# Three small products of a fused attention and MLP kernel: the second factor as a per-partition scalar operand

## The chip, the core and the metric

The kernel runs on one core of a Trainium2 chip. Its engines work side by side, each through its own queue in order: PE (TensorE, matrix products), DVE (VectorE), ACT (ScalarE), POOL (GpSimd), and SP (SyncE), whose queue here only issues transfers. The metric is the device time of one execution in microseconds (us). Three executions of the kernel before took 630.42 us (median), between 629.82 and 632.25.

## The reference

Three stages run one after the other. The first is an attention in which a query sees only the keys of its own cluster, the second an MLP with a gate, the third an MLP whose activation is a softmax-weighted value followed by a layer norm. The change lies in the third, of which this is the whole computation:

```python
h = x @ w_in                                  # 1536 x 512 times 512 x 1024
h_max = np.max(h, axis=-1, keepdims=True)
e = np.exp(h - h_max)
sm = e / (np.sum(e, axis=-1, keepdims=True) + 1e-09)
solu = h * sm
mu = np.mean(solu, axis=-1, keepdims=True)
var = np.mean((solu - mu) ** 2, axis=-1, keepdims=True)
ln = (solu - mu) / np.sqrt(var + 1e-06) * g_ln
return (ln @ w_out).astype(np.float32)        # 1536 x 1024 times 1024 x 512
```

## The kernel before

The attention and the first layer are put in order by a planner with costs and due times; the change doesn't touch them. The third stage is written out in the order in which each engine is to run it. Its 1536 tokens are 12 tiles of 128 (t = 0 to 11). All operands of the products are split into a high and a low f16 half, so each product takes three matmuls, and the values in PSUM still carry a power of two that is taken out by a scale, r, one number per partition.

For a tile t the work is in four functions:

- `products(t)` (L1365): 24 matmuls on PE, which fill two PSUM tiles h of 128x512.
- `solu(t, hs)`, first part. DVE takes the maximum of each half, negated (L1376, twice), and the smaller of the two (L1378), and multiplies it by r (L1379): this is nm. ACT computes exp(r*h + nm) with its sum (L1383, twice). DVE adds the sums (L1385), takes the reciprocal (L1388), multiplies it by r (L1389), and multiplies exp, this factor and h (L1392, twice); then the mean mu (L1396).
- `solu(t, hs)`, second part. ACT squares and sums (L1402), DVE makes the variance (L1404), POOL its power -1/2 (L1406), DVE scales it (L1407) and normalises (L1408, 128x1024). ACT copies the result to f16, the high half (L1410), and POOL subtracts that from the full value, the low half (L1412, two inputs of 128x1024 f32 and f16 in SBUF). For the last tile DVE does this subtraction.
- `flip(t, lh)` transposes both halves by two DMAs from SP's queue (L1420); for the last tile PE transposes them (L1425) and DVE copies them out of PSUM (L1426). `store(t, lT)` is 24 matmuls (L1441, for the last tile twice 24 of half the width), a copy out of PSUM on ACT (L1449) and the DMA to the output (L1450).

`factor(t)` makes the scale r once for every three tiles (L1356), in four calls.

The loop at L1487 runs, for each t, `products(t)`, then `flip(t - 2)` and `store(t - 3)`, then all of `solu(t)`. On PE the 24 matmuls of `products(t)` therefore stand right ahead of the 24 of `store(t - 3)`. On ACT the copy L1449 of tile t - 3 stands behind L1410 of tile t - 1 and ahead of the two L1383 of tile t. On DVE the maxima L1376 of tile t stand right behind L1408 of tile t - 1. On SP the output DMA of tile t - 2 stands ahead of the two transposing DMAs of tile t. Tiles 0 and 1 are computed earlier, between parts of the second stage, and for the last tile the second part of `solu` comes one turn later.

Of the kernel before, what the change touches and what calls it, by code (L numbers as in the profile page):

```python
# [15 lines left out]
ALU = mybir.AluOpType  # L16
# [5 lines left out]
def kernel(  # L22
# [21 lines left out]
    nc = tc.nc  # L44
# [82 lines left out]
    def scalar():  # L127
        i = n_scl[0]
        n_scl[0] += 1
        return scl[:, i:i + 1]  # L130
# [650 lines left out]
    def values():  # L781
# [45 lines left out]
        a = add(dict(PE=0.1), XDUE, longest_sum, after=[a], take="ex")  # L827
        add(dict(DVE=1.1), XDUE, lambda t, a=a: x_power(a), after=[a, scales["v"]], frees=a)
        T["VF"] = add(dict(DVE=0.1), 8, lambda t: factor(), after=list(scales.values()))
        for p in range(NH // 2):  # L830

# [465 lines left out]
    w2 = Weight(2, w2_in, "w2", reg1[:, 0:10])  # L1297
# [8 lines left out]
    rho, rho2, rests = [], {}, []  # L1306
# [44 lines left out]
    def factor(t):  # L1351

        n = t * P // TB
        if n not in rho2:
            rho2[n] = scalar()
            nc.vector.tensor_tensor(out=rho2[n], in0=rho[n], in1=w2.i, op=ALU.mult)  # L1356
        return rho2[n]

    def products(t):
# [11 lines left out]

    def solu(t, hs):
        r = factor(t)
        m2 = s_p.tile([P, 2], F32, tag="m2", name="m2")
        for h, _, i in hs:
            nc.vector.tensor_reduce(out=m2[:, i], in_=h, op=ALU.max, axis=AX.X, negate=True)  # L1376
        nm = s_p.tile([P, 1], F32, tag="nm2", name="nm2")
        nc.vector.tensor_reduce(out=nm, in_=m2, op=ALU.min, axis=AX.X)  # L1378
        nc.vector.tensor_tensor(out=nm, in0=nm, in1=r, op=ALU.mult)  # L1379
        e = slots[:, t % NL, :]  # L1380
        sm = s_p.tile([P, 2], F32, tag="sm2", name="sm2")
        for h, s, i in hs:
            nc.scalar.activation(e[:, s], h, AF.Exp, bias=nm, scale=r, accum_out=sm[:, i])  # L1383
        ri = s_p.tile([P, 1], F32, tag="ri2", name="ri2")
        nc.vector.tensor_scalar(  # L1385
            out=ri, in0=sm[:, 0:1], scalar1=sm[:, 1:2], scalar2=1e-9, op0=ALU.add, op1=ALU.add
        )
        nc.vector.reciprocal(ri, ri)  # L1388
        nc.vector.tensor_tensor(out=ri, in0=ri, in1=r, op=ALU.mult)  # L1389
        tot = s_p.tile([P, 2], F32, tag="tot", name="tot")  # L1390
        for h, s, i in hs:
            nc.vector.scalar_tensor_tensor(  # L1392
                out=e[:, s], in0=e[:, s], scalar=ri, in1=h, op0=ALU.mult, op1=ALU.mult, accum_out=tot[:, i]
            )
        mu = s_p.tile([P, 1], F32, tag="mu", name="mu")
        nc.vector.tensor_scalar(  # L1396
            out=mu, in0=tot[:, 0:1], scalar1=tot[:, 1:2], scalar2=-1.0 / FF2, op0=ALU.add, op1=ALU.mult
        )
        yield
        ln = slots[:, NL + t % NL, :]  # L1400
        vs = s_p.tile([P, 1], F32, tag="vs", name="vs")
        nc.scalar.activation(ln, e, AF.Square, bias=mu, accum_out=vs)  # L1402
        va = s_p.tile([P, 1], F32, tag="va2", name="va2")
        nc.vector.tensor_scalar(out=va, in0=vs, scalar1=1.0 / FF2, scalar2=1e-6, op0=ALU.mult, op1=ALU.add)  # L1404
        rs = s_p.tile([P, 1], F32, tag="rs", name="rs")
        nc.gpsimd.tensor_tensor(out=rs, in0=va, in1=mhalf, op=ALU.pow)  # L1406
        nc.vector.tensor_scalar_mul(rs, rs, LN)  # L1407
        nc.vector.tensor_scalar(out=ln, in0=e, scalar1=mu, scalar2=rs, op0=ALU.add, op1=ALU.mult)  # L1408
        lh = halves[:, t % NL]
        nc.scalar.copy(lh[:, 0], ln)  # L1410
        low = nc.gpsimd if t < NT - 1 else nc.vector
        low.tensor_tensor(out=lh[:, 1], in0=ln, in1=lh[:, 0], op=ALU.subtract)  # L1412
        lns[t] = lh
        yield
# [39 lines left out]
    def early(c):  # L1454

        if 0 < c < 3:
            while w2.done < w2.n:
                advance(fill)
            for _ in solu(c - 1, products(c - 1)):
                pass  # L1460
# [26 lines left out]
    for t in range(2, NT + 4):  # L1487
        hs = products(t) if t < NT else None
        if t == 2:
            rests.pop()()  # L1490
        part = store(t - 3, lts.pop(t - 3)) if 0 <= t - 3 < NT else iter(())
        if t >= NT:
            next(part, None)
        if t - 2 < NT:
            lts[t - 2] = flip(t - 2, lns[t - 2])
        if t == NT:
            next(last)
        for _ in part:
            pass
        if hs:  # L1500
            last = solu(t, hs)
            next(last)
            if t < NT - 1:
                next(last)
# [30 lines left out]
```

## Time and profile before

| | |
|---|---|
| Median of three runs | 630.42 us (629.82 to 632.25) |
| The profiled execution's own time | 631.68 us |
| Its span, first to last instruction | 629.9 us |
| Busy in the span: PE, DVE, ACT, POOL | 604.0, 456.9, 391.8, 250.0 us |
| Share of the span | 96%, 73%, 62%, 40% |

The profile is one execution. A row of the timeline gives the start from the span's beginning, the duration, the engine, the source line, the operation, what is written and read with shapes, the number of instructions merged into the row, and in brackets how long the engine had been idle and who ended that. A row of a source line gives the minimum, median and maximum duration of its instructions. Matmul ends are modelled: 24 matmuls of 512 columns are shown as 5.34 us, and the next group starts 5.18 us after them. The third stage without the work of the second is the stretch from 508.96 us to the end.

### The profile page before, as it was taken

How to read it: one execution, taken by the hardware profiler on the slowest of the kernel's cores; microseconds unless marked ns; L12 is line 12 of the kernel's file. 1: busy time of each engine (PE TensorE's matmuls, PEld its weight loads, DVE VectorE, ACT ScalarE, POOL GpSimd, SP SyncE). 2: the span in 40 equal slices, each digit the busy share in tenths (PEclk: the TensorE clock that was granted, in tenths of full speed). 3: DMA queues.
4: the chain of work that ended last, by engine and by line, in shares of the span. 5: the costliest groups of instructions: out<-in, count | busy, mean ns of one | idle time of the engine just before them, and what ended most of it. 6: DMA issues, size and time to landing. Idle time of an engine off the chain costs nothing. (4 is left out here: it accounts for less than half of the span.)

```text
span 629.9 us, 12832 instructions
## 1 busy us (share of the span) xinstructions
PE 604.0 (96%) x4879; PEld 395.5 (63%) x4879; DVE 456.9 (73%) x1003; ACT 391.8 (62%) x782; POOL 250.0 (40%) x215
## 2 busy tenths in 40 slices
PE   7989999999999989999999999999999999999977
PEld 6767787888888765556654666666665544444424
DVE  6878989999898858999988033566866356566662
ACT  3589998999999986678777035435335334443432
POOL 8139998758678971224221015200000212222220
PEclk9998999999999999999999999999999999999989
DMA  5897977879797116444520000260500312524241
GB/s 139 203 234 154 211 150 172 191 168 192 163 189 166 44 39 169 143 139 163 170 99 1 1 2 2 67 199 3 167 1 1 34 34 54 98 50 101 51 101 50
DMA packets 78786, 67.93 MB, mean 108 GB/s; under 512 B 61642, under 2 KB 64548, under 8 KB 78724
## 3 DMA queue, kind: packets, MB, share of 16 engines
q1 hardware_dynamic: 78724, 67.11, 44.9%
q8 instruction: 38, 0.62, 0.4%
q14 instruction: 24, 0.20, 0.1%
HBM read 34.64 MB, written 3.15 MB: 60 GB/s over the span
## 5 line engine op out<-in xcount | busy, mean ns | idle before, releaser
L976 POOL TENSOR_TENSOR ph<-p,ph 128x512 f16<-128x512 f32 x115 | 139.4, 1233 | 49.2 <-ACT ph L972 28.4
L1316 PE MATMUL yps<-g,reg 128*128 128x384 f16 x768 | 127.6, 326 | 1.0 <-DVE reg L232 0.9
L1156 PE MATMUL hps<-xT,reg 128*128 128x384 f16 x768 | 126.2, 326 | 1.5 <-DVE g L1167 1.5
L1316 PEld LDWEIGHTS <-reg 128*128 128x128 f16 x768 | 74.7, 98 | 52.4 <-DVE reg L232 4.4
L1156 PEld LDWEIGHTS <-reg 128*128 128x128 f16 x768 | 75.0, 98 | 50.5 <-issue 1.7
L914 DVE TENSOR_REDUCE nma<-sm 128x1 f32<-128x512 f32 x144 | 96.3, 680 | 8.4 <-PE sm L903 7.8
L1177 POOL TENSOR_TENSOR g<-g,g 128x384 f16<-128x384 f32 x40 | 41.7, 1044 | 123.8 <-ACT g L1172 123.8
L967 ACT ACTIVATE p<-st 128x512 f32<-128x512 f32 x114 | 68.6, 609 | 6.4 <-PE st L959 5.2
L958 PE MATMUL st<-OP 128*128 128x256 f32 (+1 forms) x191 | 69.3, 374 | 2.5 <-ACT p L967 1.3
L1406 POOL TENSOR_TENSOR rs<-va,mhalf 128x1 f32<-128x1 f32 x12 | 6.6, 551 | 158.9 <-DVE va L1404 158.9
L972 ACT CAST ph<-p 128x512 f16<-128x512 f32 x109 | 67.4, 630 | 0.4
L1365 PE MATMUL h<-reg,xT 128*128 128x512 f16 x288 | 64.1, 379 | 0.0
L959 PE MATMUL st<-OP 97*128 97x512 f32 (+3 forms) x191 | 63.0, 342 | 0.0
L995 PE MATMUL av<-vh,ph 128*128 128x65 f16 x576 | 61.1, 195 | 1.6 <-POOL ph L976 1.6
L991 PE MATMUL av<-vh,ph 128*128 128x65 f16 x576 | 61.9, 194 | 0.0
L994 PE MATMUL av<-vh,ph 128*128 128x64 f16 x576 | 61.2, 193 | 0.0
L991 PEld LDWEIGHTS <-ph 128*128 128x128 f16 x576 | 52.8, 99 | 11.2 <-issue 9.5
L903 PE MATMUL sm<-OP 80*128 80x512 f32 x192 | 57.6, 361 | 1.6 <-DVE nma L914 0.8
L1441 PEld LDWEIGHTS <-g 128*128 128x128 f16 x312 | 30.7, 99 | 39.0 <-DMA g<-g 6.6
L995 PEld LDWEIGHTS <-ph 128*128 128x128 f16 x576 | 53.6, 97 | 2.0 <-POOL ph L976 2.0
L994 PEld LDWEIGHTS <-ph 128*128 128x128 f16 x576 | 53.7, 97 | 0.2
L208 ACT ACTIVATE junk<-reg 128x512 bf16<-128x512 f32 x48 | 30.4, 633 | 30.8 <-DVE reg L198 18.6
(193 smaller groups left out, 1067.6 us busy)
## 6 DMA issues: line engine op xcount, KB each, us to landing
OP<-hl SPq DMA_DIRECT2D x48, 384.0 KB
raw<-in_moe_w_in_dram SPq DMA_DIRECT2D x24, 512.0 KB
raw<-in_moe_w_out_dram SPq DMA_DIRECT2D x24, 512.0 KB
xT<-in_v_dram SPq DMA_DIRECT2D x8, 384.0 KB
out_dram<-ob SPq DMA_DIRECT2D x11, 256.0 KB
raw<-in_k_dram SPq DMA_DIRECT2D x14, 192.0 KB
raw<-in_q_dram SPq DMA_DIRECT2D x14, 192.0 KB
OP<-oht SPq DMA_DIRECT2D x30, 48.0 KB
```

What stands on the lines that cost most here:

```text
L914: nc.vector.tensor_reduce(out=out, in_=src, op=ALU.max, axis=AX.X, negate=True)
L958: nc.tensor.matmul(t["tile"][:, at], K2[:, ks], Q2[:, cs], start=True, stop=False)
L959: nc.tensor.matmul(t["tile"][:, at], K1[0:n, ks], Q1[0:n, cs], start=False, stop=True)
L967: nc.scalar.activation(p32s[u, m], t["tile"], AF.Exp, scale=SCALE)
L972: e(phs[u, m][:, 0], p32s[u, m])
L976: e.tensor_tensor(out=phs[u, m][:, 1], in0=p32s.pop((u, m)), in1=phs[u, m][:, 0], op=ALU.subtract)
L991: nc.tensor.matmul(av[:, i, :], ph[:, 0, qs], vh[:, u, kt, D:], start=(m == 0 and i == 0), stop=False,)
L994: nc.tensor.matmul(av[:, i, 0:D], ph[:, 0, qs], vh[:, u, kt, 0:D], start=False, stop=False)
L995: nc.tensor.matmul(av[:, i, :], ph[:, 1, qs], vh[:, u, kt, D:], start=False, stop=(m == NU - 1 and kt == NJ - 1 and i == NJ - 1),)
L1156: nc.tensor.matmul(self.ps, w1.at(c, m, e), xT[:, x, c, n * TB:(n + 1) * TB], start=(c == 0 and e == x), stop=(c == ND - 1 and e == 1),)
L1316: nc.tensor.matmul(yps, wo.at(f, c, e), lp["g", n][:, x, f, :], start=(f == 0 and e == x), stop=(f == NF - 1 and e == 1),)
L1365: nc.tensor.matmul(h, xT[:, x, c, t * P:(t + 1) * P], w2.half(i * ND + c, e), start=(c == 0 and e == x), stop=(c == ND - 1 and x == 1),)
```

## The change

In `factor` and in two places of `solu`, a product of two 128x1 columns was a `tensor_tensor`, which reads both columns as tensors. It is now a `tensor_scalar_mul`, which reads one column as a tensor and the other as a scalar operand with one value per partition. The number and the order of the instructions on every engine stay as they were: 28 DVE instructions (4 at L1356, 12 at L1379, 12 at L1389) have another operation.

```diff
@@ factor(t)
             rho2[n] = scalar()
-            nc.vector.tensor_tensor(out=rho2[n], in0=rho[n], in1=w2.i, op=ALU.mult)
+            nc.vector.tensor_scalar_mul(rho2[n], rho[n], w2.i)
@@ solu(t, hs)
         nc.vector.tensor_reduce(out=nm, in_=m2, op=ALU.min, axis=AX.X)
-        nc.vector.tensor_tensor(out=nm, in0=nm, in1=r, op=ALU.mult)
+        nc.vector.tensor_scalar_mul(nm, nm, r)
...
         nc.vector.reciprocal(ri, ri)
-        nc.vector.tensor_tensor(out=ri, in0=ri, in1=r, op=ALU.mult)
+        nc.vector.tensor_scalar_mul(ri, ri, r)
```

## Rows read from the trace of the kernel before

**Rows 1.** Waits of PE from 520 to 630: who for whom, total, times, longest

```profile
PE ops__8220 L1441 <- DMA g<-g: 4.6, 2, 4.3
```

**Rows 2.** Timeline of PE: products of tile 11, stores of tiles 8 and 9

```profile
591.84 5.34 PE L1365 MATMUL h<-reg,xT 128*128 128x512 f16 x24
597.02 5.34 PE L1441 MATMUL ops__8134<-reg,g 128*128 128x512 f16 x24
602.20 5.60 PE L1441 MATMUL ops__8180<-reg,g 128*128 128x512 f16 x24
```

**Rows 3.** Timeline of DVE: the maxima of tiles 2 and 3

```profile
513.32 1.28 DVE L1376 TENSOR_REDUCE m<-h 128x1 f32<-128x512 f32 x2
...
522.17 1.28 DVE L1376 TENSOR_REDUCE m<-h 128x1 f32<-128x512 f32 x2
```

**Rows 4.** Two changed lines: durations minimum/median/maximum in ns, first and last start

```profile
L1379 DVE TENSOR_TENSOR nm<-nm,scl x12: 159/1896/1933, 484.0 to 608.1; 128x1 f32<-128x1 f32 x12
...
L1389 DVE TENSOR_TENSOR ri<-ri,scl x12: 159/159/161, 486.3 to 612.2; 128x1 f32<-128x1 f32 x12
```

**Rows 5.** Timeline of all engines, tile 8: from the maxima to exp

```profile
574.95 1.28 DVE L1376 TENSOR_REDUCE m<-h 128x1 f32<-128x512 f32 x2
...
576.24 2.13 POOL L1412 TENSOR_TENSOR g<-g,g 128x1024 f16<-128x1024 f32 x1 [2.25 <-issue]
...
576.45 1.93 DVE L1379 TENSOR_TENSOR nm<-nm,scl 128x1 f32<-128x1 f32 x1
...
578.42 0.78 ACT L1383 ACTIVATE g<-h,nm,scl 128x512 f32<-128x512 f32 x1 [1.72 <-DVE nm L1379]
```

**Rows 6.** Timeline, three earlier places: small TENSOR_SCALAR on DVE beside POOL

```profile
275.40 1.14 POOL L1177 TENSOR_TENSOR g<-g,g 128x384 f16<-128x384 f32 x1 [2.23 <-ACT g L1172]
...
276.17 0.20 DVE L1137 TENSOR_SCALAR scl<-scl 128x1 f32<-128x1 f32 x1
...
218.70 3.89 POOL L976 TENSOR_TENSOR ph<-p,ph 128x512 f16<-128x512 f32 x3
...
221.15 0.15 DVE L143 TENSOR_SCALAR scl<-scl 128x1 uint32<-128x1 uint32 x1
...
65.38 1.61 POOL L769 TENSOR_TENSOR vh<-xT,vh 128x768 f16<-128x768 f32 x1
...
66.42 0.59 DVE L1010 TENSOR_SCALAR ri<-ri,scl 128x6 f32<-128x6 f32 x1
```

**Rows 7.** Two TENSOR_SCALAR lines: L1385 with a scalar column, L1407 with a constant

```profile
L1385 DVE TENSOR_SCALAR ri<-sm x12: 212/214/215, 485.8 to 611.7; 128x1 f32<-128x1 f32 x12
...
L1407 DVE TENSOR_SCALAR rs<-rs x12: 154/154/155, 490.3 to 616.2; 128x1 f32<-128x1 f32 x12
```

**Rows 8.** Timeline of all engines, from the maxima of tile 11 on

```profile
606.61 1.28 DVE L1376 TENSOR_REDUCE m<-h 128x1 f32<-128x512 f32 x2
...
607.69 0.68 ACT L1449 ACTIVATE ob<-ops__8134,scl 128x512 f32<-128x512 f32 x1
...
608.82 2.68 SPq L1420 DMA_TRANSPOSE g<-g  x2
...
610.08 0.78 ACT L1383 ACTIVATE g<-h,nm,scl 128x512 f32<-128x512 f32 x1 [1.71 <-DVE nm L1379]
...
612.12 1.04 PE L1441 MATMUL ops__8220<-reg,g 128*128 128x512 f16 x2 [4.32 <-DMA g<-g]
...
613.47 5.44 PE L1441 MATMUL ops__8220<-reg,g 128*128 128x512 f16 x16 [0.31 <-DMA g<-g]
...
618.36 1.23 DVE L1412 TENSOR_TENSOR g<-g,g 128x1024 f16<-128x1024 f32 x1 [1.11 <-ACT g L1410]
...
621.40 2.78 PE L1441 MATMUL ops__8268<-reg,g 128*128 128x256 f16 x24
...
624.27 0.47 ACT L1449 ACTIVATE ob<-ops__8268,scl 128x256 f32<-128x256 f32 x1 [1.93 <-PE ops__8268 L1441]
```

**Rows 9.** Stretches: us, busy PE, PEld, DVE, ACT, POOL, PE clock, DMA, GB/s

```profile
607.00:612.00 5.00, 0.80 (x4) 0.19 (x2) 3.20 (x6) 3.00 (x6) 2.12 (x1) 0.83 0.55 127
612.00:614.00 2.00, 1.57 (x4) 0.39 (x5) 1.89 (x7) 0.00 (x0) 0.00 (x0) 0.50 0.41 76
```

## The prediction

> **What bounds the kernel now.** I read the page first, then PE's waits in the last stage, then the timeline by tile, and last the changed lines. On the page PE is busy 96% of the span, and from 520 us on PE waits only for the transposing DMA of tile 10, 4.6 us in two waits near the end [rows 1]. So one might call PE the bound. The timeline says otherwise for the last tiles. PE runs `products(t)` and `store(t - 3)` in turn, 5.18 us each (591.84, 597.02, 602.20), 10.36 us for a tile [rows 2]. DVE starts the maxima of tile 3 at 522.17 and those of tile 11 at 606.61: 84.44 us for eight tiles, 10.56 each [rows 3, 8]. PE had the products of tile 11 done at 591.84 + 5.34 = 597.2, and DVE comes to them 9.4 us later. PE runs ahead on work that it has in stock, and pays for it at the end, when it stands until 612.12 because tile 10 isn't normalised and transposed yet [rows 8]. From tile 3 on, the loop through DVE and ACT is what sets the end, not PE.
>
> **What the loop holds.** From tile 2 to tile 3 the maxima are 522.17 - 513.32 = 8.85 us apart [rows 3], later 10.56. The changed line L1379 explains the difference: of its 12 instructions the shortest takes 159 ns and the median 1896 [rows 4]. The timeline of tile 8 shows why. POOL's subtraction L1412 of the tile before starts at 576.24 and ends at 578.37; L1379, a product of 128x1, starts 0.21 us later and ends at 578.38, with it [rows 5]. ACT's exp waits for it and starts at 578.42. L1379 is held for as long as POOL's instruction runs. The median says that at least half of the tiles are held so; in the timeline it is nine of them, tiles 3 to 11, since for tiles 0 to 2 no subtraction runs at that moment. L1389, the same operation at a time when POOL is idle, takes 159 to 161 ns in all 12 cases.
>
> **The change part by part.** The question is whether the new form is held too.
>
> Rows bearing on it: L1137, an f32 TENSOR_SCALAR of 128x1 with a scalar column as the new ones have, takes 0.20 us at 276.17, while POOL's TENSOR_TENSOR runs from 275.40 to 276.54 [rows 6]. L143, 128x1 with a constant, takes 0.15 us at 221.15 inside three POOL subtractions that run without a gap from 218.70 to 222.59 [rows 6]. Against them stands L1010, a TENSOR_SCALAR of 128x6 with a scalar column: 0.59 us at 66.42, ending at 67.01 as POOL's subtraction ends at 66.99 [rows 6]. Wide ones are held, those of one element per partition are not, as far as these rows go.
>
> [...]
>
> The price of the new form itself: 0.154 us with a constant (L1407), 0.214 us with a scalar column (L1385) [rows 7], against 0.159 before. These are the two ends, -0.005 and +0.055 us an instruction. I take +0.055, since the new operand is a scalar column. Held, L1379 costs 1.93 us; free, 0.21. Each of nine tiles loses 1.72 us of the loop.
>
> L1356, four times 0.15 us before tiles 0, 3, 6 and 9, is on the loop in front of a tile and costs 4 x 0.055 = 0.2 us at most. Once PE sets the pace the slack of the loop hides this. L1389 stands between exp and the end of the tile: it costs 0.055 us, hidden by the same slack in every tile but the last.
>
> **What is late next.** Without the hold the DVE loop takes 8.85 + 2 x 0.055 = 8.96 us a tile, less than PE's 10.36, so something that goes with PE takes over. In the last tile's terms:
>
> - DVE alone: exp of tile 3 would start at 522.17 + 1.50 (from the maxima to L1379, as 574.95 to 576.45 [rows 5]) + 0.21 + 0.04 = 523.9, and exp of tile 11 eight loops later at 595.6.
> - ACT's order: the copy L1449 of tile t - 3 stands ahead of exp of tile t (before: 607.69, then 610.08 [rows 8]). It needs the store's matmuls, and PE runs these right behind `products(t)`. For tile 11 they end at 597.02 + 5.34 = 602.36 [rows 2]. ACT follows a PE group after 0.09 us (621.40 + 2.78 = 624.18, start 624.27 [rows 8]): L1449 from 602.45 to 603.13, exp of tile 11 from 603.1.
>
> The later one counts: 603.1 in place of 610.08, **7.0 us earlier**. The floor lies 10.36 us apart for successive tiles and the free loop 8.96, so counting back from tile 11 (7.5 us of distance, 1.4 lost per tile) the floor is in force from tile 6 on; the gain is limited by it and not by nine times 1.72 = 15.5 us.
>
> From exp of tile 11 to the end the chain has no other supplier: sums, L1392, square, variance, normalising, copy, the last subtraction (618.36 to 619.59), PE's transposes and the stores. It moves as a whole, less 0.055 us for L1389: 6.9 us. What could hold it up is PE's store of tile 10. PE is free of tile 9's store at 602.20 + 5.34 = 607.5. Tile 10's transposing DMA is issued 1.13 us after the start of L1449 (607.69 to 608.82 [rows 8]), so at 602.45 + 1.13 = 603.6; its first half lets PE go 3.30 us later and its second half 4.65 us later (612.12, 613.47 [rows 8]), at 606.9 and 608.2. The remaining 16 of the 18 matmuls ahead of the transposes are done at 608.2 + 16 x 0.216 = 611.7, with 0.216 = 5.18 / 24. The low half of tile 11 is ready at 619.59 - 6.9 = 612.7. PE is there first by 1 us, less the first eight transposes (at most 0.6). So nothing is lost there.
>
> **The sum.** Span 629.9 - 6.9 = 623.0, the profiled execution 631.68 - 6.9 = 624.8. The median of the runs shown lies 1.26 us under that execution: 630.42 - 6.9 = 623.5 us.
>
> **The rivals.**
>
> 1. The hold stays: a TENSOR_SCALAR of one element takes the shared path as the 128x6 one did. Place: L1379 beside L1412 in nine tiles. The DVE loop stays the bound, and each tile pays 2 x 0.055 us, 9 x 0.11 = 1.0 us: **631.4 us**, slower than before. It decides from the point at which one element per partition is held at all. For it: L1010. Against it: L1137 and L143. The change then does nothing but swap the operation. I give it 10%.
> 2. PE was the bound all along, and only the last tile's own 1.72 us, on the chain behind the last products, come off: **628.7 us**. For it: PE's 96% and no PE wait before the end. Against: 9.4 us between PE's end and DVE's start on tile 11, and the two pitches. 4%.
> 3. The gain comes but PE's clock takes half of it back. [...] In the forecast PE still stands about 0.4 us ahead of tile 10's second half. [...] 6%.
>
> **How the numbers follow.** The forecast has 80%: 623.5 us, 1.1% less. A difference under 0.5% (3.2 us) can't be told from none in a measurement of this kernel. Forecast and rival 3 lie beyond it on the fast side; rivals 1 and 2 inside it, rival 1 with a little chance of more. Faster 0.86, same 0.12, slower 0.02. The forecast's own spread: 0.4 us of the floor on ACT and of PE's end towards faster, 1 us in tile 10's transposes towards slower, and 1 us for the median of a few runs, since the three shown are spread over 2.4 us. With rival 3 taken in on the upper side, the range is 621.8 to 626.5.
>
> **What would show it.** In the profile of the changed kernel L1379 should take 0.15 to 0.22 us in all 12 cases, also while L1412 runs. The pitch of the maxima should be about 8.9 us for tiles 3 to 5 and 10.36 after, with ACT's exp waiting no longer for DVE but starting right behind L1449, which then waits for PE. Exp of tile 11 should start near 603.1, PE should wait under 1 us for tile 10's DMA where it waited 4.6, and the clock of 612 to 616 should read near 1. The forecast is wrong if L1379 still shows 1.9 us (rival 1), if it is short and the pitch stays at 10.56 (a new wait in the loop), or if PE starts tile 10's store early and slowly (rival 3).

## Result and profile after

The changed kernel takes 625.6 us (median of 20 runs, 623.53 to 631.09), the kernel before, measured beside it, 632.12 us (20 runs, 629.82 to 636.73). The ratio is 0.9897, with a 95% interval of 0.9876 to 0.9918: 1.0% faster, or 6.5 us, between 5.2 and 7.8. The forecast was 623.5 us, 6.9 us less. The profiled execution has a span of 622.7 us, where the forecast had 623.0.

First the two changed lines, minimum/median/maximum in ns; they answer to [rows 4].

```profile
L1379 DVE TENSOR_SCALAR nm<-nm,scl x12: 212/214/216, 483.5 to 600.8; 128x1 f32<-128x1 f32 x12
...
L1389 DVE TENSOR_SCALAR ri<-ri,scl x12: 212/214/215, 485.8 to 604.6; 128x1 f32<-128x1 f32 x12
```

L1379 is short in all 12 tiles. L1389, which was never held, has become 0.055 us longer. The wait of ACT's exp for L1379 is gone. Before, it was this (total, number of waits, longest):

```profile
ACT g L1383 <- DVE nm L1379: 15.5, 9, 1.8
```

Now tile 8 in the timeline after, from the maxima to exp; this answers to [rows 5].

```profile
568.20 1.28 DVE L1376 TENSOR_REDUCE m<-h 128x1 f32<-128x512 f32 x2
...
569.49 2.12 POOL L1412 TENSOR_TENSOR g<-g,g 128x1024 f16<-128x1024 f32 x1 [2.25 <-issue]
...
569.70 0.21 DVE L1379 TENSOR_SCALAR nm<-nm,scl 128x1 f32<-128x1 f32 x1
...
570.84 0.69 ACT L1449 ACTIVATE ob<-ops__7881,scl 128x512 f32<-128x512 f32 x1 [1.49 <-PE ops__7881 L1441]
...
571.43 0.77 ACT L1383 ACTIVATE g<-h,nm,scl 128x512 f32<-128x512 f32 x1
```

POOL's subtraction still runs for 2.12 us, and L1379 starts 0.21 us after it, as before. It now ends 1.70 us ahead of POOL. The wait of ACT has a new name: exp stands behind the copy L1449, and that waits 1.49 us for PE's store.

The maxima of tiles 3, 4, 7, 8 and 11 on DVE show two phases of the loop, where it was 10.56 us a tile before [rows 3, 8].

```profile
521.80 1.28 DVE L1376 TENSOR_REDUCE m<-h 128x1 f32<-128x512 f32 x2
...
530.69 1.28 DVE L1376 TENSOR_REDUCE m<-h 128x1 f32<-128x512 f32 x2
...
557.83 1.28 DVE L1376 TENSOR_REDUCE m<-h 128x1 f32<-128x512 f32 x2
568.20 1.28 DVE L1376 TENSOR_REDUCE m<-h 128x1 f32<-128x512 f32 x2
...
599.28 1.28 DVE L1376 TENSOR_REDUCE m<-h 128x1 f32<-128x512 f32 x2
```

From tile 3 to tile 4 it is 8.89 us, from tile 7 to tile 11 (599.28 - 557.83) / 4 = 10.36 on average, PE's pitch. Tile 11 starts 7.3 us earlier than before (606.61, [rows 8]).

The end, all engines, answers to the rest of [rows 8], and the wait of PE (first row) to [rows 1].

```profile
PE ops__8220 L1441 <- DMA g<-g: 0.9, 2, 0.7
```

```profile
601.92 0.69 ACT L1449 ACTIVATE ob<-ops__8134,scl 128x512 f32<-128x512 f32 x1 [1.48 <-PE ops__8134 L1441]
602.51 0.77 ACT L1383 ACTIVATE g<-h,nm,scl 128x512 f32<-128x512 f32 x1
...
603.06 3.53 SPq L1420 DMA_TRANSPOSE g<-g  x2
...
607.22 0.60 PE L1441 MATMUL ops__8220<-reg,g 128*128 128x512 f16 x2 [0.20 <-DMA g<-g]
...
608.52 3.63 PE L1441 MATMUL ops__8220<-reg,g 128*128 128x512 f16 x16 [0.70 <-DMA g<-g]
...
610.83 1.23 DVE L1412 TENSOR_TENSOR g<-g,g 128x1024 f16<-128x1024 f32 x1 [1.11 <-ACT g L1410]
...
611.99 1.06 PE L1425 MATMUL trl<-id,g 128*128 128x128 f16 x16
...
612.88 1.46 PE L1441 MATMUL ops__8220<-reg,g 128*128 128x512 f16 x6
```

The last row, the rest of tile 10's store behind the transposes, was this in the kernel before:

```profile
620.10 1.46 PE L1441 MATMUL ops__8220<-reg,g 128*128 128x512 f16 x6
```

PE's wait has gone from 4.6 to 0.9 us, and 16 matmuls take 3.63 us where they took 5.44. The stretch around the wait shows the clock, as in [rows 9] (us, busy PE, PEld, DVE, ACT, POOL, clock, DMA, GB/s): 1.00 after, 0.50 before.

```profile
607.00:609.00 2.00, 1.10 (x6) 0.36 (x6) 0.40 (x3) 0.87 (x2) 0.55 (x1) 1.00 0.47 86
```

**A yardstick for the experiments.** Ahead of tile 3, about the first 508 us, no changed instruction was held (they took 0.150 to 0.161 us each there before, 0.202 to 0.216 after), and the length of that part varies by up to 7 us between the profiles below. So I also compare the time from the first matmul of tile 3's products (start of its row on PE) to the end of the span. I call it the stage. Before it is 629.9 - 508.96 = 120.94 us; after, 622.7 - 508.44 = 114.26 us: 6.7 us less. Of the 7.2 us by which the spans differ, 0.5 lie ahead of the stage. Each stage comes from one profile; the changed kernel's two differ by 0.4 us, so differences of that size say nothing by themselves.

| kernel | tile 3 starts | span | stage | ratio to before (95%) |
|---|---|---|---|---|
| before | 508.96 | 629.9 | 120.9 | |
| the change | 508.44 | 622.7 | 114.3 | 0.9897 (0.9876 to 0.9918) |
| only L1379 | 511.53 | 625.6 | 114.1 | 0.9888 (0.9848 to 0.9928) |
| all but L1379 | 507.39 | 628.8 | 121.4 | 0.9987 (0.9965 to 1.0009) |
| last two tiles | 509.32 | 627.4 | 118.1 | 0.9948 (0.9923 to 0.9973) |
| all tiles but the last | 506.99 | 621.4 | 114.4 | 0.9857 (0.9822 to 0.9891) |
| one input in PSUM | 510.14 | 624.5 | 114.4 | 0.9895 (0.9839 to 0.9950) |
| scalar form, 2 columns | 509.82 | 630.8 | 121.0 | 1.0002 (0.9969 to 1.0035) |
| scalar form, 3 columns | 509.32 | 630.3 | 121.0 | 0.9991 (0.9965 to 1.0017) |
| copy late | 510.19 | 624.5 | 114.3 | 0.9877 (0.9839 to 0.9915) |
| copy late, DMA early | 509.55 | 622.5 | 113.0 | 0.9865 (0.9827 to 0.9903) |
| the change again | 513.91 | 628.6 | 114.7 | 0.9905 (0.9867 to 0.9942) |

### The profile page after: what moved, and what is told of

Same layout as the page of the kernel before. It is cut to its first block, busy times and chain, and to the rows that moved or that the text cites. A ratio compares the mean times of both kernels' runs of the same rounds, so it can differ in the third digit from the quotient of the medians.

```text
span 622.7 us, 12832 instructions
## 1 busy us (share of the span) xinstructions
PE 601.1 (97%) x4879; PEld 394.5 (63%) x4879; DVE 442.3 (71%) x1003; ACT 391.1 (63%) x782; POOL 250.0 (40%) x215
## 4 chain that ended last, share of the span: by engine, by line
PE 46%; DVE 10%; ACT 3%; issue 2%; DMA 1%; SPq 0%; ACTq 0%
PE yps L1316 19%; PE h L1365 10%; PE hps L1156 8%; DVE reg L198 2%; DVE g L1167 2%; DVE reg L232 1%; DVE reg L194 1%; DVE hps L1167 1%; DVE g L1177 1%; DVE reg L189 1%; ACT reg L229 1%; PE ops__8134 L1441 1%; PE ops__8050 L1441 1%; PE ops__7965 L1441 1%; PE ops__7881 L1441 1%
## 5 line engine op out<-in xcount | busy, mean ns | idle before, releaser
L1156 PE MATMUL hps<-xT,reg 128*128 128x384 f16 x768 | 127.9, 329 | 1.6 <-DVE g L1167 1.6
```

The source lines that it names most:

```text
L1156: nc.tensor.matmul(self.ps, w1.at(c, m, e), xT[:, x, c, n * TB:(n + 1) * TB], start=(c == 0 and e == x), stop=(c == ND - 1 and e == 1),)
```

## Experiments

**Which of the three lines.** Two kernels split the change.

```diff
 only L1379:
-        nc.vector.tensor_tensor(out=nm, in0=nm, in1=r, op=ALU.mult)
+        nc.vector.tensor_scalar_mul(nm, nm, r)
 all but L1379: the edits at L1356 and L1389, and L1379 as before
```

> Only L1379 (the product of the maximum with the scale) takes the scalar operand; L1356 and L1389 stay tensor products. My theory (L1379 was held behind POOL's L1412 for 1.7 us in nine tiles, the DVE loop set the end): the whole gain, 6.5 to 7 us, ratio about 0.9895; L1379 at 0.21 us in all tiles. Rival (the gain is spread over all 28 replaced instructions, or comes from L1389 and L1356): a part of it, under 4 us.

> L1356 and L1389 take the scalar operand, L1379 stays a tensor product. My theory: no gain, L1379 still 1.9 us in tiles 3 to 11; 9 x 0.055 = 0.5 us slower for the scalar operand at L1389, which a measurement can't tell from none. Rival (gain from these two lines): 3 us or more faster.

L1379 alone gives all of it: 0.9888, and 114.1 us in the stage. The other two lines give nothing: 0.9987, an interval that holds 1, and a stage that is 0.5 us longer, which fits 9 x 0.055 but is about what two profiles of one kernel differ by. From the maxima of tile 3 to those of tile 11 that kernel takes 605.48 - 520.70 = 84.78 us where the kernel before takes 84.44, 0.34 more where 8 x 0.055 makes 0.44. L1379 is held in that kernel as it was.

```profile
L1379 DVE TENSOR_TENSOR nm<-nm,scl x12: 159/1866/1930, 482.4 to 607.0; 128x1 f32<-128x1 f32 x12
```

**Loop or last tile.** If PE were the bound, the hold would count in the last tile alone.

```diff
-        nc.vector.tensor_tensor(out=nm, in0=nm, in1=r, op=ALU.mult)
+        if t >= NT - 2:            # the other kernel: t < NT - 1
+            nc.vector.tensor_scalar_mul(nm, nm, r)
+        else:
+            nc.vector.tensor_tensor(out=nm, in0=nm, in1=r, op=ALU.mult)
```

> L1379 takes the scalar operand in tiles 10 and 11 alone. My theory: the DVE loop sets the end in every tile, so each freed tile gives 1.67 us (1.72 less 0.05): 2 x 1.7 = 3.4 us faster, ratio 0.9946. Rival (PE is the bound and only the chain of the last tile counts): 1.7 us faster, ratio 0.997.

> L1379 takes the scalar operand in all tiles but the last, which keeps the tensor product. My theory: the loop catches up before the last tile, and there exp waits for ACT's copy of an older tile anyway; the changed kernel has nm ready 1.5 us ahead of exp, so a hold that ends with L1412 (602.7 in the changed kernel's profile) delays exp by about 0.2 us: 6.5 to 7 us faster, within 0.5 us of the full change. Rival (only the last tile's hold counts): no gain.

Freeing all tiles but the last gives the full gain (114.4 us), which refutes the last tile's hold as the cause. By the times it gives even more, 0.9857, 6.9 to 11.3 us; its stage doesn't show more than the full change. The added lines move what stands behind them by three: L1382 is the product of L1379, L1452 the copy L1449, L1386 the exp L1383. DVE of that kernel shows the last tile held for its 1.93 us, and ACT's exp behind it at 601.25, 0.08 us after the copy's end (in the changed kernel it starts 0.1 us ahead of that end): the hold is still there and costs about 0.1 to 0.2 us.

```profile
599.28 1.93 DVE L1382 TENSOR_TENSOR nm<-nm,scl 128x1 f32<-128x1 f32 x1
...
600.48 0.69 ACT L1452 ACTIVATE ob<-ops__8134,scl 128x512 f32<-128x512 f32 x1 [1.54 <-PE ops__8134 L1444]
...
601.25 0.78 ACT L1386 ACTIVATE g<-h,nm,scl 128x512 f32<-128x512 f32 x1
```

Freeing the last two gives 2.9 us in the stage, more than one tile's 1.7, and less than the 3.4 expected. The ratio, 0.9948, fits 3.3 us, but its interval reaches from 1.7 to 4.9 us and tells nothing here. Exp of tile 11 is where the theory puts it: 606.96 - 509.32 = 97.6 us after tile 3's products begin, 3.5 us earlier than before (610.08 - 508.96 = 101.1). The rest is lost on PE. These are exp of tile 11, PE's store of tile 10, and the stretch in which its second part starts.

```profile
606.96 0.78 ACT L1386 ACTIVATE g<-h,nm,scl 128x512 f32<-128x512 f32 x1
...
610.70 0.73 PE L1444 MATMUL ops__8220<-reg,g 128*128 128x512 f16 x2 [2.62 <-DVE g L1395]
612.03 4.81 PE L1444 MATMUL ops__8220<-reg,g 128*128 128x512 f16 x16 [0.60 <-DMA g<-g]
...
616.68 1.06 PE L1428 MATMUL trl<-id,g 128*128 128x128 f16 x16
```

```profile
612.00:614.00 2.00, 1.97 (x5) 0.73 (x6) 1.00 (x3) 0.27 (x2) 0.55 (x1) 0.50 0.00 0
```

PE had stood for 2.6 us (the row names a DVE instruction that ended just then, but PE starts 3.30 us after the issue of tile 10's transposing DMAs at 607.40, as before, 608.82 to 612.12 [rows 8], so I take these for what it waited for). From 612 to 614 the granted clock is 0.50, where the changed kernel has 1.00 during this store, and the 16 matmuls take 4.81 us, 1.2 us more than the 3.63 of the changed kernel; the transposes come behind them. I read the missing 0.6 us (3.5 less 2.9) as this. No run took the low clock away alone, so its share is argued, not shown.

**What is held: the operation or the second input.** In one kernel the product stays a TENSOR_TENSOR and one input moves. The product stands at L1380 there.

```diff
-        nc.vector.tensor_reduce(out=nm, in_=m2, op=ALU.min, axis=AX.X)
-        nc.vector.tensor_tensor(out=nm, in0=nm, in1=r, op=ALU.mult)
+        low_ = ps_c.tile([P, 512], F32, tag="acc", name="nmp")[:, 0:1]      # PSUM
+        nc.vector.tensor_reduce(out=low_, in_=m2, op=ALU.min, axis=AX.X)
+        nc.vector.tensor_tensor(out=nm, in0=low_, in1=r, op=ALU.mult)
```

> L1379 stays a tensor product, but the minimum (L1378) is written to PSUM, so that only one of the two inputs lies in SBUF. My theory (what is held is the second input from SBUF): L1379 under 0.3 us in all tiles, 6 to 7 us faster. Rival (the operation tensor_tensor is held, wherever its inputs lie): L1379 still 1.9 us, time as before.

```profile
L1380 DVE TENSOR_TENSOR nm<-nmp,scl x12: 157/159/159, 485.2 to 602.4; 128x1 f32<-128x1 f32 x12
```

The tensor product with one input in PSUM takes 0.16 us in all tiles, and the stage is 114.4 us. POOL's subtraction stands in that kernel as it did. In the changed kernel it starts 0.13 us after ACT's copy of the high half ends (600.45 to 600.58); with one input in PSUM that copy ends at 602.08 for tile 10, and tile 11's product starts at 602.4. By that estimate the two run side by side, as before. The operation alone wasn't held (0.16 us); with both its tensor inputs in SBUF it was (1.86 to 1.93 us in tiles 3 to 11 before).

**How wide may the scalar form be.** The edit writes the product two or three times, side by side; exp reads the first column. The product stands at L1380 here too.

```diff
-        nc.vector.tensor_tensor(out=nm, in0=nm, in1=r, op=ALU.mult)
+        wide = s_p.tile([P, 2], F32, tag="nmw", name="nmw")                 # or 3
+        nc.vector.tensor_scalar_mul(wide, nm.to_broadcast([P, 2]), r)
+        nm = wide[:, 0:1]
```

> L1379 is a product with a scalar operand as in the change, but over two columns (the minimum read twice, written to 128x2). Theory from the rows (one element per partition is free, wider ones take the second path as the 128x6 did): held, 1.9 us in tiles 3 to 11, time as before or up to 0.5 us more. Rival (the scalar form of such small width is free as such): 0.22 us, 6 to 7 us faster.

> The same over three columns. [...]

The first row is the kernel with two columns, the second that with three.

```profile
L1380 DVE TENSOR_SCALAR nmw<-nm,scl x12: 228/1902/1942, 484.8 to 609.1; 128x2 f32<-128x2 f32 x12
```

```profile
L1380 DVE TENSOR_SCALAR nmw<-nm,scl x12: 228/1900/1942, 484.3 to 608.6; 128x3 f32<-128x3 f32 x12
```

Both are held for 1.9 us, and the gain is gone (1.0002 and 0.9991, 121.0 us). One column more, and the change would have done nothing. POOL's subtraction of tile 7 ends at 579.31 with two columns and at 578.82 with three, the product of tile 8 beside it at 579.34 and 578.84. So 2 and 3 columns were held here, and the 6 of L1010, 0.59 us and ending 0.02 us after POOL's instruction [rows 6]; 1 column was not, 0.212 to 0.216 us at L1379 after the change and 0.20 at L1137 [rows 6]. What makes the difference is not shown.

**What sets the end now.** Two variants of the changed kernel, and the changed kernel once more.

```diff
 copy late: on ACT the copy L1449 of tile t - 3 behind the two exp of tile t
+        if hs:
+            last = solu(t, hs)
+            next(last)
         for _ in part:
             pass
         if hs:
-            last = solu(t, hs)
-            next(last)
             if t < NT - 1:
...
 DMA early, besides: tile 10's transposing DMAs ahead of tile 8's output DMA
-        if t - 2 < NT:
+        if t - 2 < NT and t - 2 not in lts:
...
+        if t == NT - 1:
+            lts[t - 1] = flip(t - 1, lns[t - 1])
         for _ in part:
```

> The changed kernel with ACT's copy L1449 of tile t - 3 put behind the two exp of tile t, not ahead of them. My theory (in the changed kernel exp waits for this copy, and the copy for PE's store): exp of tile 11 starts about 4.4 us earlier than in the changed kernel, right behind nm, but tile 10's transposing DMAs still stand behind the output DMA of tile 8, so PE's store of tile 10 starts as late as before: end at most 0.3 us earlier, time as the changed kernel. Rival (exp of the last tile alone sets the end): 4 us faster than the changed kernel.

> The same, and tile 10's transposing DMAs issued ahead of tile 8's output DMA. My theory: PE no longer waits at the end, 1.2 to 1.4 us less from the products of tile 3 to the end than the changed kernel: 0.2%, at the edge of what a measurement tells. Rival (the end hangs on something else by now): no difference from the changed kernel.

> The changed kernel itself, on the chip of the two variants: 6.5 to 7 us faster than before. Products of tile 3 to the end: 114.3 us, as in its first profile.

With the copy late, exp of tile 11 starts at 599.67, 89.5 us after tile 3's products, where the changed kernel has 602.51 - 508.44 = 94.1: 4.6 us earlier, right behind nm. The stage is as long as before it, 114.3 us, since PE still waits 1.0 us for tile 10's DMA.

```profile
599.67 0.78 ACT L1383 ACTIVATE g<-h,nm,scl 128x512 f32<-128x512 f32 x1 [1.61 <-DVE nm L1379]
...
604.82 3.61 SPq L1420 DMA_TRANSPOSE g<-g  x2
...
609.05 0.60 PE L1441 MATMUL ops__8220<-reg,g 128*128 128x512 f16 x2 [0.28 <-DMA g<-g]
610.33 3.63 PE L1441 MATMUL ops__8220<-reg,g 128*128 128x512 f16 x16 [0.67 <-DMA g<-g]
```

With the DMA early as well, PE runs the last three stores (that of tile 8 starts at 597.60) without a wait.

```profile
602.78 5.34 PE L1441 MATMUL ops__8182<-reg,g 128*128 128x512 f16 x24
607.96 4.05 PE L1441 MATMUL ops__8220<-reg,g 128*128 128x512 f16 x18
611.85 1.06 PE L1425 MATMUL trl<-id,g 128*128 128x128 f16 x16
```

The stage is 113.0 us, 1.3 us under the changed kernel's first profile and 1.7 under its second. The times don't settle it: medians of 624.29 against 626.79 us on that chip, and intervals of the ratios to before that overlap. By the profile this kernel beats both; by the times it is only no worse. The changed kernel's second measurement, 0.9905, agrees with its first (0.9897); its stage is 114.7 us, 0.4 above what was expected.

## Why the prediction was right

- **The hold.** L1379 was to take 0.15 to 0.22 us in 12 tiles; it takes 0.212 to 0.216. That the old form is held for its second tensor input from SBUF and the new one is free for its single column is shown from both sides: one input in PSUM frees the old form (0.16 us), a second column holds the new one (1.90 us). That POOL's subtraction is what holds it rests on the rows: before, L1379 ends within 0.02 us of L1412 in all nine held tiles, and takes 0.16 us in the three where none runs. No run moved the subtraction. The path that rival 1 and the expectation for two columns speak of is the author's picture of the hold: the traces show how long the instructions take, not where they meet. Rival 1 is out: no product of one column was held after the change, 0.216 us at most.
- **The price of the scalar operand.** +0.055 us an instruction, as measured at L1389 (159 to 214 ns). In the loop it is too small to be told apart with any certainty.
- **The bound.** DVE's loop, not PE, set the end of the kernel before: freeing all tiles but the last brings the whole gain. Rival 2 is out, in spite of PE's 96%. (From 520 us on PE also waits 0.3 us for tile 11's last subtraction, which the prediction's first paragraph leaves out; nothing hangs on it.)
- **The new floor.** From tile 6 on exp was to wait for ACT's copy. The first L1449 that waits for PE is that ahead of tile 6's exp, at 550.12; from tile 7 on the wait is 1.5 us. The pitch was 8.89 to 9.01 from tile 3 to tile 6 and 10.36 from tile 7 on, forecast 8.96 and 10.36. Exp of tile 11 was forecast 7.0 us earlier; measured from tile 3's products it is 101.1 - 94.1 = 7.0.
- **The end.** This term was mis-sized. It was to move as a whole, 6.9 us; it moved 6.7. Tile 10's transposing DMA let PE start 4.16 us after its issue (603.06 to 607.22), 3.30 forecast from [rows 8], and its second half 5.46 us after it, 4.65 forecast. So PE comes from tile 10's store to the transposes at 612.0, just when tile 11's low half is ready (610.83 + 1.23 = 612.06), and not 1 us ahead of it: the first eight transposes, of the high half, are still to be done then. The rest of that store starts 0.82 us after the low half is ready (612.88), before it was 0.51 (620.10 - 619.59): 0.3 us are lost there, where the prediction had nothing. The end hangs on PE and this DMA, no longer on tile 11's own chain. The run with the late copy shows it: exp 4.6 us earlier moves nothing.
- **Rival 3.** PE stood for 0.9 us in place of 0.4 (1.3 us in the changed kernel's second profile), and the granted clock stayed at 1.00, from 612 to 616 too. The rival is no fancy: after 2.6 us of idle, in the kernel with the last two tiles free, the clock was 0.50 from 612 to 614, and in the kernel before after 4.3 us [rows 8, 9]. The size that the prediction gives it, 626.5 us against 623.5, counts 3 us for it, and no run shows a loss of 3 us. What they show is 16 matmuls of tile 10's store in 3.63 us at a clock of 1.00, and in 4.81 and 5.44 us where it was 0.50 for a part of them: 1.2 us more with the last two tiles free, 1.8 in the kernel before.
- **The absolute time.** 623.5 was worked out from 630.42, a median of three; over 20 runs the kernel before has 632.12. Of the 2.1 us between forecast and result 1.7 are this, and 0.4 the gain. The prediction allowed 1 us for the median of a few runs and 1 us for the transposes, so up to 625.5 by itself; the 625.6 lies in the range because rival 3's 626.5 was taken in, and rival 3 didn't happen. That the absolute time was within the range is partly luck; the gain of 6.5 us is not.

## What to carry to other kernels

When a tiny DVE instruction lasts microseconds, look at what POOL runs beside it, and at where the inputs of DVE's instruction lie. Here the POOL instruction was always a subtraction with two inputs from SBUF, 2.12 to 2.13 us long at L1412; others weren't tried. Beside it a 128x1 product was held with both tensors in SBUF (1.86 to 1.93 us), and free with one of them in PSUM (0.16) or as a scalar form of one column (0.21); as a scalar form of two or three columns it was held (1.94 in tile 8 of both). When such a hold goes, work out the next wait in the order of each queue; here it capped 15 us of freed loop at 7.

## What the runs showed of the hardware that was not expected

Tile 10's two transposing DMAs occupied SP's queue for 2.68 us before and for 3.53, 3.61 and 3.98 us in three profiles of the changed order (changed kernel, late copy, changed kernel again); with all tiles but the last free it was 3.75. The pairs of tiles 2 to 9 took 2.64 to 2.68 us in the kernel before and in the changed one. That is 0.9 to 1.3 us more, just where PE waits. Issued ahead of tile 8's output DMA, they ended at 600.93, the last two of four that took 7.12 us with the pair of tile 9 (from 593.81 on), and PE didn't wait for them. What delays them was not tried; it stays open.
